# Decayed block attention followed by a two-layer MoE: attention by chunk over all heads, interleaved with both MoE layers on every engine; k transpose sharing the k-v matmul; smelu from one relu pass

## The chip, the cores and the metric

One core of one Trainium2 chip. The metric is the device time of the whole program in microseconds (us). An execution is timed several times; "span" is the length of one profiled execution, about 1.8 us shorter than the time of the same execution. Engines: PE (matmul), PEld (its weight loads), DVE (VectorE), ACT (ScalarE), POOL (GpSimd), SP (which here only asks for DMA transfers).

## The reference

```python
# attention: q, k, v are (4, 8, 768, 64) float32, lam one decay per head, near 1
for b in range(nb):                      # blocks of 64 tokens
    intra = (qb @ kb.T * Dmask) @ vb     # Dmask = lam ** (i - j) where i >= j, else 0
    inter = (qb * lam_pow) @ kv_state
    out[:, :, sl] = intra + inter
    kv_state = lam_block * kv_state + (kb * rev_pow).T @ vb
# MoE layer (one expert): x is (3072, 512)
h = x @ w_in                             # 512 -> 2048
g = np.where(h >= 1, h, np.where(h <= -1, 0.0, (h + 1) ** 2 / 4))   # smelu
y = g @ w_out                            # 2048 -> 512
```

The block size is free: the decay can be folded into q and k as powers of lam. Both kernels work on chunks of 128 tokens, in bfloat16 on PE.

## The kernel before

Attention runs first, one batch and one pair of heads at a time over all six chunks; only when all of x is there does the MoE run, in six stripes of 512 tokens. The framework's scheduler sets the order on each engine.

```python
    w_in_sb = big.tile([128, KO, d_ff], BF16)
    nc.gpsimd.dma_start(out=w_in_sb, in_=...)           # both weights, whole, first of all
    w_out_sb = big.tile([128, FO, d_model], BF16)
    nc.gpsimd.dma_start(out=w_out_sb, in_=...)
    ...
        for b in range(B):
            for hp in range(H // 2):                    # 16 head pairs
                # load q, k, v of the pair; scale q and k on ACT; k again on DVE
                # 12 PE transposes of 128x128, copied back by DVE
                kvp = kvpool.tile([128, 128], BF16, name="kvp", tag="kv")   # running k-v state
                for g in range(NG):
                    # 4 score matmuls of 64 rows; DVE multiplies by the causal mask
                    for bi in range(GRP):
                        nc.tensor.matmul(po[:, bi, :, :], lhsT=v_bf[:, blk, :], rhs=sc[:, bi, :, :], ...)
                        # two matmuls of 128 columns with kvp, then
                        nc.tensor.matmul(pkv, lhsT=kdd2[:, blk, :], rhs=v_bf[:, blk, :], ...)
                        for hi in range(2):
                            nc.vector.scalar_tensor_tensor(out=kvp[...], in0=kvp[...],
                                scalar=lamblk[...], in1=pkv[...], op0=AX.mult, op1=AX.add)
    ...
        for ms in range(NMS):                           # 6 stripes of 512 tokens
            for ni in range(FO):                        # layer 1: 16 x 4 matmuls of 512 columns
                ...
                nc.scalar.activation(out=tt, in_=ph, func=AF.Relu, scale=0.5, bias=chalf[:, 0:1])
                nc.scalar.activation(out=cc, in_=ph, func=AF.Relu, scale=1.0, bias=cm1[:, 0:1])
                nc.vector.tensor_single_scalar(aa, tt, 1.0, AX.min)
                nc.vector.tensor_tensor(a2, aa, aa, op=AX.mult)
                nc.vector.tensor_tensor(gT[:, ni, :], a2, cc, op=AX.add)
            for msub in range(MSTRIPE // 128):          # layer 2: 4 x 16 matmuls of 512 columns
                ...
```

## Time and profile before

358.08 us, median of 3 runs (358.08 to 358.14). Three parts of the span:

| part | from, us | to, us | what limits it |
|---|---|---|---|
| loads | 0 | 44 | q and k behind both weights |
| attention | 44 | 174 | PE, DVE and the k-v state waiting for each other |
| MoE | 174 | 356 | PE, and DVE in layer 1: 29.5 us for each stripe |

From the page of the kernel before: busy time of each engine, then the span in 40 slices of 8.9 us, in tenths.

```profile
PE 293.7 (82%) x1504; PEld 135.5 (38%) x1504; DVE 222.2 (62%) x693; ACT 203.0 (57%) x403; POOL 29.5 (8%) x44
...
PE   0011668888888888888999999999999999999995
...
DVE  0010678888888888888588078248518807825850
ACT  7112625544445555532399199369649729937951
...
PEclk9999999999999999999999999999999999999999
DMA  7999999878777734431000200110020020011011
```

PE starts late, is at 8 with DVE at 8 through the attention, and at 9 in the MoE. The chain of waits of the kernel before, its first 45 us (start, length, what):

```profile
3.68 10.29 SPq L121
...
14.01 4.87 SPq L124
...
18.91 4.96 SPq L121
...
26.44 4.99 SPq L121
```

Lines 121 and 124 ask for q and k. SP's queue is blocked for up to 10.3 us at a time, while the two weight loads (both asked for by 4 us) hold the DMA engines, which the page shows at 9.

How fast PE really streams is not in its busy time; it is in the distance between starts. PE's timeline of the kernel before, at the end of the attention (start, length, instruction):

```profile
174.08 0.31 PE L192 MATMUL po<-qTp,kvp 128*128 128x128 bf16 x1
174.19 0.42 PE L185 MATMUL po<-sc,v_bf 128*128 128x256 bf16 x1
174.40 0.32 PE L196 MATMUL pkv<-v_bf,kdd_1917 128*128 128x128 bf16 x1
174.51 1.49 PE L227 MATMUL ph<-xT,w_in_sb 128*128 128x512 bf16 x3
```

The 128-column matmul takes 0.11 us to the next start, the 256-column one 0.21, three 512-column ones 1.28: half the rate of the MoE later, where starts of 512 columns are 0.216 us apart. The PEclk row stays at 9 through both. Last, the costs of the old activation, from the groups of the kernel before (busy us, mean ns of one, after the bar):

```profile
L236 ACT ACTIVATE cc<-ph,cm_82 128x512 bf16<-128x512 f32 x96 | 77.3, 806 | 0.0
L233 ACT ACTIVATE tt<-ph,chalf 128x512 bf16<-128x512 f32 x96 | 76.7, 799 | 1.0 <-PE ph L227 0.9
L239 DVE TENSOR_SCALAR aa<-tt 128x512 bf16<-128x512 bf16 x96 | 27.6, 287 | 51.5 <-ACT tt L233 51.5
```

These lengths overlap: two passes start 0.57 us apart. Per 512 columns of layer 1, ACT needs 1.14 us and DVE 1.19 us, PE 0.86.

### The profile page before, as it was taken

What the parts mean: (1) busy time and instruction counts of PE and PEld (TensorE: products, weight loads), DVE (VectorE), ACT (ScalarE), POOL (GpSimd) and SP (SyncE); (2) the same over time, 40 slices, a digit from 0 to 9 for tenths busy, and PEclk for the clock granted to TensorE, in tenths of its full rate; (3) what the DMA queues carried; (4) which work ended last, traced back from release to release, by engine and by line L of the source; (5) the groups of instructions that cost most, each with busy time, mean ns of one, the idle gap of its engine ahead of it and who ended that gap; (6) DMA issues with size and microseconds to landing.
All of it is one profiled execution on the core that took longest, in us unless ns stands there. A gap on an engine that the chain in (4) does not pass through costs nothing.

```text
span 356.3 us, 4688 instructions
## 1 busy us (share of the span) xinstructions
PE 293.7 (82%) x1504; PEld 135.5 (38%) x1504; DVE 222.2 (62%) x693; ACT 203.0 (57%) x403; POOL 29.5 (8%) x44
## 2 busy tenths in 40 slices
PE   0011668888888888888999999999999999999995
PEld 0010334444444444443443443344344344344432
DVE  0010678888888888888588078248518807825850
ACT  7112625544445555532399199369649729937951
POOL 7000011111222221110000000000000000000000
PEclk9999999999999999999999999999999999999999
DMA  7999999878777734431000200110020020011011
GB/s 144 201 196 178 205 205 204 129 111 120 110 112 110 111 26 27 28 23 14 2 0 0 90 30 0 62 59 0 29 90 1 0 90 30 0 61 60 0 53 66
DMA packets 81481, 26.53 MB, mean 74 GB/s; under 512 B 75824, under 2 KB 77872, under 8 KB 81456
## 3 DMA queue, kind: packets, MB, share of 16 engines
q1 hardware_dynamic: 53776, 18.88, 23.6%
q0 software_dynamic: 27680, 7.34, 20.5%
q8 instruction: 12, 0.20, 0.2%
q14 instruction: 13, 0.11, 0.1%
HBM read 27.27 MB, written 6.29 MB: 94 GB/s over the span
## 4 chain that ended last, share of the span: by engine, by line
DVE 40%; PE 33%; SPq 11%; ACT 8%; issue 5%; DMA 1%; DVEq 0%; ACTq 0%
PE py L247 19%; DVE kvp L200 11%; DVE gT L242 8%; SPq L121 7%; PE po L185 5%; DVE aa L239 4%; ACT cc L236 4%; SPq L124 4%; DVE sc L177 3%; PE po L189 3%; PE psc L172 3%; ACT tt L233 3%; DVE kTp L158 3%; DVE qTp L158 2%; PE po L192 2%
## 5 line engine op out<-in xcount | busy, mean ns | idle before, releaser
L247 PE MATMUL py<-w_out_sb,gT 128*128 128x512 bf16 x384 | 93.8, 380 | 2.6 <-DVE gT L242 2.2
L227 PE MATMUL ph<-xT,w_in_sb 128*128 128x512 bf16 x384 | 94.0, 385 | 0.7
L236 ACT ACTIVATE cc<-ph,cm_82 128x512 bf16<-128x512 f32 x96 | 77.3, 806 | 0.0
L233 ACT ACTIVATE tt<-ph,chalf 128x512 bf16<-128x512 f32 x96 | 76.7, 799 | 1.0 <-PE ph L227 0.9
L211 ACT CAST xT<-po 64x256 bf16<-64x256 f32 x96 | 35.1, 366 | 70.7 <-PE po L192 70.2
L239 DVE TENSOR_SCALAR aa<-tt 128x512 bf16<-128x512 bf16 x96 | 27.6, 287 | 51.5 <-ACT tt L233 51.5
L227 PEld LDWEIGHTS <-w_in_sb 128*128 128x128 bf16 x384 | 37.8, 99 | 50.1 <-issue 10.8
L247 PEld LDWEIGHTS <-gT 128*128 128x128 bf16 x384 | 35.5, 98 | 53.5 <-DVE gT L242 14.0
L154 PE MATMUL ptr<-ident,qkdd 128*128 128x128 bf16 x192 | 30.6, 303 | 28.1 <-ACT qkdd L133 21.0
L253 ACT COPY osb<-py 128x512 f32<-128x512 f32 x24 | 13.9, 586 | 49.5 <-PE py L247 49.5
L172 PE MATMUL psc<-qTp,kTp 64*128 64x128 bf16 x192 | 30.9, 296 | 11.8 <-DVE kTp L158 7.2
L185 PE MATMUL po<-sc,v_bf 128*128 128x256 bf16 x96 | 35.9, 408 | 5.1 <-DVE sc L177 2.7
L177 DVE TENSOR_TENSOR sc<-psc,causalT 128x256 bf16<-128x256 f32 x96 | 37.7, 420 | 2.2
L127 POOL DMA_DIRECT2D v_bf<-in_v_dram x32 | 26.2, 827 | 129.4 <-PE pkv L196 117.2
L154 PEld LDWEIGHTS <-qkdd 128*128 128x128 bf16 x192 | 20.9, 136 | 35.2 <-ACT qkdd L133 21.2
L189 PE MATMUL po<-qTp,kvp 128*128 128x128 bf16 x80 | 23.6, 295 | 6.1 <-DVE kvp L200 5.1
L192 PE MATMUL po<-qTp,kvp 128*128 128x128 bf16 x80 | 25.1, 314 | 0.0
L172 PEld LDWEIGHTS <-kTp 64*128 64x128 bf16 x192 | 11.3, 106 | 32.5 <-issue 19.3
L189 PEld LDWEIGHTS <-kvp 128*128 128x128 bf16 x80 | 8.7, 109 | 22.7 <-DVE kvp L200 19.9
L185 PEld LDWEIGHTS <-v_bf 128*128 128x128 bf16 x96 | 10.6, 123 | 16.7 <-DVE sc L177 15.6
L158 DVE COPY qTp<-ptr 128x512 bf16<-128x512 bf16 (+1 forms) x32 | 11.3, 357 | 0.9
L158 DVE COPY kTp<-ptr 128x512 bf16<-128x512 bf16 (+1 forms) x32 | 11.1, 353 | 0.9 <-PE ptr L154 0.5
(326 smaller groups left out, 252.5 us busy)
## 6 DMA issues: line engine op xcount, KB each, us to landing
qk_nat<-in_q_dram SPq DMA_DIRECT2D x32, 192.0 KB, 4.0
qk_nat<-in_k_dram SPq DMA_DIRECT2D x32, 192.0 KB, 4.1
out_dram<-osb SPq DMA_DIRECT2D x24, 256.0 KB, 2.2
v_bf<-in_v_dram POOLq DMA_DIRECT2D x32, 96.0 KB, 3.3
w_in_sb<-in_moe_w_in_dram POOLq DMA_DIRECT2D x1, 2048.0 KB, 16.1
w_out_sb<-in_moe_w_out_dram POOLq DMA_DIRECT2D x1, 2048.0 KB, 28.3
lam_b<-in_lam_dram SPq DMA_DIRECT2D x1, 4.0 KB, 2.6
```

Source lines behind the costliest of these rows:

```text
L154: nc.tensor.transpose(out=ptr[:, c, :], in_=qkdd[:, base + c, off:off + 128], identity=ident)
L158: nc.vector.tensor_copy(dst[:, base:base + nchk, :], ptr[:, :nchk, :])
L172: nc.tensor.matmul(psc[:, bi, :], lhsT=kTp[ps:ps + 64, blk, :], rhs=qTp[ps:ps + 64, blk, :], start=True, stop=True)
L177: nc.vector.tensor_tensor(out=sc[:, :, hi, :], in0=psc, in1=_ins(causalT, 1, GRP), op=AX.mult)
L185: nc.tensor.matmul(po[:, bi, :, :], lhsT=v_bf[:, blk, :], rhs=sc[:, bi, :, :], start=True, stop=first)
L189: nc.tensor.matmul(po[:, bi, 0, :], lhsT=kvp, rhs=qTp[:, blk, :], start=False, stop=False)
L200: nc.vector.scalar_tensor_tensor(out=kvp[ps:ps + 64, ps:ps + 64], in0=kvp[ps:ps + 64, ps:ps + 64], scalar=lamblk[h0 + hi][ps:ps + 64, 0:1] ...
L227: nc.tensor.matmul(ph, lhsT=w_in_sb[:, ko, ni * 128:(ni + 1) * 128], rhs=xT[:, ko, m0:m0 + MSTRIPE], start=(ko == 0), stop=(ko == KO - 1))
L233: nc.scalar.activation(out=tt, in_=ph, func=AF.Relu, scale=0.5, bias=chalf[:, 0:1])
L236: nc.scalar.activation(out=cc, in_=ph, func=AF.Relu, scale=1.0, bias=cm1[:, 0:1])
L239: nc.vector.tensor_single_scalar(aa, tt, 1.0, AX.min)
L247: nc.tensor.matmul(py, lhsT=gT[:, ko, msub * 128:(msub + 1) * 128], rhs=w_out_sb[:, ko, :], start=(ko == 0), stop=(ko == FO - 1))
```

## The change

The intent is to have no attention phase at all. A unit of attention is one 128-token chunk and half the heads; there are 48. The first four chunks (8 units) run alone; the others are slotted between the MoE matmuls. All decay goes into two tables over the whole sequence, so the state U is a plain running sum. The order on every engine is written by hand. Both weights come in four slices each, after the first q, k and v. The matmul that makes the k-v product also transposes k: its moving operand is v beside an identity. The core of what is added (cut and shortened, with remarks; what it replaces is the code above):

```diff
+    ctx.enter_context(tc.manual_schedule())
...
+        nc.gpsimd.tensor_tensor(t, qf, _bc(tab_q[:, cb, :], 2, D), op=AX.mult)     # qs, on POOL
+        k_eng.tensor_tensor(t, kf, _bc(tab_k[:, cb, :], 2, D), op=AX.mult)         # ks: DVE for chunks 0-3, then POOL
+        nc.scalar.copy(out=vi[c % NV][:, :, 0, :], in_=vf...)                      # v beside the identity
+    def stage_t(u):        # 2 q transposes, 2 matmuls of 256 columns: k-v product and k transpose
+            nc.tensor.transpose(out=pq[:, j, :], in_=qs[c][...], identity=ident)
+            nc.tensor.matmul(pk[:, j], lhsT=ks[c][...], rhs=vi[c % NV][:, hp], start=True, stop=True)
+        # ACT: two copies of q into a block-diagonal tile, one of kT; DVE: U = U + pk
+    def stage_s(u):        # 2 score matmuls of 256 columns, DVE mask of 512
+    def stage_o(u):        # 2 or 4 matmuls of 256 columns, two ACT copies into xT
...
+        nc.scalar.activation(out=r_t[s][:, ni % 2, :], in_=ph, func=AF.Relu, bias=one[:, 0:1])
+        nc.vector.tensor_scalar(t, r, 0.5, 1.0, op0=AX.mult, op1=AX.min)           # per 1,024 columns
+        nc.vector.tensor_tensor(w, r, t, op=AX.subtract)
+        nc.vector.tensor_tensor(gT[s][:, ni - 1:ni + 1, :], w, t, op=AX.mult)
...
+    for c in range(CPS):                       # prologue: chunks 0 to 3
+        ensure_cast(c, nc.vector)
+        if c >= 1:
+            load_w_in(state["wi"]); state["wi"] += 1
+        # four attention steps
+    load_w_in(state["wi"])
+    for i in range(WS):
+        load_w_out(i)
+    ensure_loaded(CPS + 1)
+    ensure_cast(CPS)                           # chunk 4
+    # one more attention step: t of unit 8 and o of unit 7
...
+    for s in range(NST + 1):                   # step i: layer 1 of stripe s, layer 2 of stripe s - 1
+        for i in range(FO):
+            l1(s, i)            # 4 matmuls of 512 columns
+            # t or s of a unit
+            smelu(s, i)
+            l2(s - 1, i)        # 4 matmuls of 512 columns
+            # o of the unit before
```

## The prediction

> **What bounds it now.** The page and the timeline show three parts of the 356.3 us span. (a) To about 44 us: load-bound. The chain of waits is the sync queue's q and k issues (one blocked 10.3 us) while both weight loads hold the DMA engines; PE's first matmul is at 20.2 us. (b) 44 to 174 us: attention. PE and DVE are each busy about 88% (windows 60-150 us: PE 78.7, DVE 79.0 of 90), but PE, DVE and the running k-v state wait for each other. PE streams slowly: starts of 128-column matmuls are 0.107 us apart, of 256-column ones 0.21, of 512-column ones still 0.43 at 175 us. (c) 174 to 356 us: MoE, 29.5 us for each 512-token stripe. PE starts a 512-column matmul every 0.216 us, so 128 of them are 27.6 us; the rest is DVE (gT) not keeping up.
>
> The doubled spacing in (b) agrees with the Trainium skill, TensorE: Matmul & The Clock Gate, "What's actually happening": 1.2 GHz until sustained busy, then 2.4. The page's PEclk row does not show it.
>
> **What changes.** Attention runs in 48 units (a 128-token chunk, half the heads). A full unit is 2 transposes and 8 matmuls of 256 columns. At warm rate, estimated from the spacings above: 2 x 0.08 + 8 x 0.11 = 1.05 us, about 48 us in all, against 166 us for the MoE's 768 matmuls. All but the first 8 units are slotted between MoE matmuls, so part (b) ceases to be a phase and its waits are covered.
>
> Other engines, from the trace's spacings: ACT 0.57 us per 512 columns from PSUM, 0.37 per 256. One relu in place of two: 96 x 0.57 = 55; attention 5 x 0.37 + 0.3 = 2.15 per unit, 103; output copies 14: 172 us. DVE: smelu per 1,024 columns 0.42 + 2 x 0.69 = 1.8, 48 times = 86; masks 48 x 0.65 = 31; state 40 x 0.38 = 15; with setup 138 us. POOL: 44 products of 128x512; the Trainium skill, GPSIMD Engine Reference, "Elementwise — side-by-side cycle accounting" gives 2.6 cycles per element at 1.2 GHz: 1.1 us each, some 50 us in all, an estimate that this trace cannot check. So PE bounds the steady part.
>
> **Sum.** Prologue 31 us: first chunk ready near 9 us (q, k, v are issued before the weights), then 8 units at about 2.5 us, a serial ACT-PE-DVE chain on a cold PE, with chunk 3's load close behind. Stripe 0 (layer 1 and 9 units, no layer 2): ACT- and DVE-bound, 31. Stripes 1 to 3: 27.6 + 8 x 1.05, plus 4% for waits, 37.4 each, 112. Stripe 4: 36. Stripe 5, no attention: 28. Last layer 2: 14; last copy and store 4. Span 256; the measured time is 1.8 longer than the span now: **258 us**, range 247 to 275. Faster by over 2%: 0.98; within 2%: 0.01; slower: 0.01.
>
> **What would show it.** PE's first matmul near 9 us; first layer-1 matmul at 29 to 35 us; PE near 9 in every slice after it save stripe 0; 512-column starts 0.216 us apart throughout; ACT busy about 70%, DVE 55%; the chain mostly PE; POOL products 1.0 to 1.5 us.
>
> **What would make it wrong.** POOL products of 2 us or more, or shutting out DVE's two-input work (prologue and stripe 0 longer). PE falling back to the cold rate in stripe 0 (up to +15 us). Single PSUM buffers for pq, pk, ps and po stalling PE at each unit: 0.3 us x 40 is +12. First-layer weight slices queued behind q/k/v (the first slices late). A prologue unit nearer 3.5 us: +8.

## The result, and the profile after

The time is 263.36 us (median of 5 runs, 263.24 to 265.2), before 358.08 (357.62 to 358.14), result correct. The ratio is 0.737 (95% interval 0.735 to 0.739). Ratios are the mean time of one kernel's fast runs over that of the other's of the same rounds, so they are not quite the ratio of the medians quoted. The profiled execution is the slowest of the five (265.2 us, span 263.5); the others have spans of 261.5 to 262.2.

The page of the changed kernel, the same rows; a slice is now 6.6 us:

```profile
PE 222.8 (85%) x1209; PEld 118.7 (45%) x1232; DVE 143.8 (55%) x245; ACT 173.7 (66%) x389; POOL 54.2 (21%) x61
...
PE   0567306666889999999999999999999999999993
...
DVE  3554201388887576657574766574747645555300
ACT  4768303778996977797779777977796754554210
...
PEclk9999755999999999999999999999999999999998
DMA  6999999999990526753574357110111011111122
```

There is work from the first slice on, then a hole near slices 5 and 6 in PE, DVE and ACT together, then a stretch (slices 7 to 12) in which PE is at 6 to 8 while ACT rises from 3 to 9, and from slice 13 on PE is at 9 to the end. The hole in the merged timeline of the changed kernel (all engines; in brackets the idle time just before, and what ended it):

```profile
34.37 1.04 POOL L156 TENSOR_TENSOR ks<-kf,tab_k 128x512 bf16<-128x512 f32 x1 [7.35 <-DMA kf<-in_k_dram]
...
40.86 0.62 ACT L158 CAST vi_152<-vf 128x512 bf16<-128x512 f32 x1 [11.87 <-DMA vf<-in_v_dram]
...
41.53 0.58 PE L173 MATMUL pk<-vi_152,ks 128*128 128x256 bf16 x2 [12.56 <-ACT vi_152 L158]
...
43.19 1.62 PE L234 MATMUL ph<-xT,w_in_sb 128*128 128x512 bf16 x3 [0.22 <-issue]
```

PE stands for 12.6 us, ACT's copy of v of chunk 4 ends the wait, and that copy had itself waited 11.9 us for the load of v; k of the same chunk was 7.4 us late before it. This is attention step 17, the one the prologue has after its four chunks. Only then does layer 1 begin, at 43.2 us.

The steady part, PE's timeline of the changed kernel from one step to the second next:

```profile
88.84 1.03 PE L234 MATMUL ph<-xT,w_in_sb 128*128 128x512 bf16 x4
89.70 0.28 PE L169 MATMUL pq<-ident,qs 128*128 128x128 bf16 x2
89.81 0.38 PE L173 MATMUL pk<-vi_152,ks 128*128 128x256 bf16 x2
90.03 1.03 PE L258 MATMUL py<-w_out_sb,gT 128*128 128x512 bf16 x4
90.90 0.27 PE L206 MATMUL po<-qbd_146,U 128*128 128x256 bf16 x1
91.00 0.27 PE L207 MATMUL po<-sc,vi_150 128*128 128x256 bf16 x1
91.11 0.27 PE L206 MATMUL po<-qbd_146,U 128*128 128x256 bf16 x1
91.22 0.27 PE L207 MATMUL po<-sc,vi_150 128*128 128x256 bf16 x1
91.33 1.03 PE L234 MATMUL ph<-xT,w_in_sb 128*128 128x512 bf16 x4
92.20 0.38 PE L192 MATMUL ps<-qbd_148,kT 128*128 128x256 bf16 x2
92.41 1.03 PE L258 MATMUL py<-w_out_sb,gT 128*128 128x512 bf16 x4
```

No line has an idle time in brackets: every matmul starts when the one before it has been streamed. Two steps with one unit take 4.44 us (88.84 to 93.28): 16 matmuls of 512 columns at 0.216 are 3.45, and the unit is the other 0.99.

The groups that answer to those of the old activation, and POOL's products, in the changed kernel:

```profile
L238 ACT ACTIVATE r<-ph,one 128x512 bf16<-128x512 f32 x96 | 65.9, 687 | 43.3 <-PE ph L234 39.6
L153 POOL TENSOR_TENSOR qs<-qf,tab_q 128x512 bf16<-128x512 f32 x24 | 25.3, 1052 | 121.7 <-PE pq L169 92.0
...
L156 POOL TENSOR_TENSOR ks<-kf,tab_k 128x512 bf16<-128x512 f32 x20 | 22.3, 1117 | 7.9 <-DMA kf<-in_k_dram 7.9
```

One pass in place of two, and POOL at 1.04 to 1.1 us for each product.

Three times cut the span into the terms of the prediction: the first layer-1 matmul (end of the prologue), the first layer-2 matmul (within a microsecond of the start of stripe 1), and the end. All are starts of records in the traces.

| | first layer 1 | first layer 2 | end | prologue | stripe 0 | rest |
|---|---|---|---|---|---|---|
| predicted | 31 | 62 | 256 | 31 | 31 | 194 |
| the changed kernel | 43.2 | 79.1 | 263.5 | 43.2 | 35.9 | 184.4 |

The total hides two errors of opposite sign: the first two terms are 17 us too small together, the third 10 us too large.

### The profile page after: what moved, and what is told of

Same layout as the page of the kernel before. It is cut to its first block, busy times and chain, and to the rows that moved or that the text cites. A ratio compares the mean times of both kernels' runs of the same rounds, so it can differ in the third digit from the quotient of the medians.

```text
span 263.5 us, 3576 instructions
## 1 busy us (share of the span) xinstructions
PE 222.8 (85%) x1209; PEld 118.7 (45%) x1232; DVE 143.8 (55%) x245; ACT 173.7 (66%) x389; POOL 54.2 (21%) x61
## 4 chain that ended last, share of the span: by engine, by line
PE 69%; DVE 3%; ACT 1%; issue 0%; ACTq 0%
PE py L258 31%; PE ph L234 26%; PE po L207 3%; PE ps L192 3%; PE pk L173 2%; PE po L206 2%; PE pq L169 1%; DVE gT L250 1%; DVE w_726 L249 1%; DVE sc L195 0%; DVE w_768 L249 0%; ACT r L238 0%; DVE U L186 0%; ACT xT L212 0%; ACT osb L262 0%
## 5 line engine op out<-in xcount | busy, mean ns | idle before, releaser
L238 ACT ACTIVATE r<-ph,one 128x512 bf16<-128x512 f32 x96 | 65.9, 687 | 43.3 <-PE ph L234 39.6
L153 POOL TENSOR_TENSOR qs<-qf,tab_q 128x512 bf16<-128x512 f32 x24 | 25.3, 1052 | 121.7 <-PE pq L169 92.0
L186 DVE TENSOR_TENSOR U<-pk,U 128x256 bf16<-128x256 f32 x32 | 13.6, 424 | 56.5 <-ACT kT L179 56.5
L195 DVE TENSOR_TENSOR sc<-ps,causal 128x512 bf16<-128x512 f32 x48 | 32.9, 685 | 4.6 <-PE ps L192 4.0
L156 POOL TENSOR_TENSOR ks<-kf,tab_k 128x512 bf16<-128x512 f32 x20 | 22.3, 1117 | 7.9 <-DMA kf<-in_k_dram 7.9
L169 PE MATMUL pq<-ident,qs 128*128 128x128 bf16 x96 | 14.3, 235 | 6.7 <-POOL qs L153 6.7
L179 ACT CAST kT<-pk 128x256 bf16<-128x256 f32 x48 | 17.9, 372 | 2.4 <-PE pk L173 1.3
L173 PE MATMUL pk<-vi_152,ks 128*128 128x256 bf16 x32 | 6.8, 298 | 14.6 <-ACT vi_152 L158 12.6
L169 PEld LDWEIGHTS <-qs 128*128 128x128 bf16 x96 | 10.1, 106 | 16.8 <-POOL qs L153 6.7
L192 PEld LDWEIGHTS <-kT 128*128 128x128 bf16 x96 | 8.5, 101 | 19.4 <-ACT kT L179 11.0
L158 ACT CAST vi_152<-vf 128x512 bf16<-128x512 f32 x8 | 4.9, 610 | 11.9 <-DMA vf<-in_v_dram 11.9
L177 ACT COPY qbd_146<-pq 64x256 bf16<-64x256 bf16 x32 | 11.6, 361 | 1.6 <-PE pq L169 1.2
L177 ACT COPY qbd_144<-pq 64x256 bf16<-64x256 bf16 x32 | 11.5, 361 | 0.6 <-PE pq L169 0.2
L177 ACT COPY qbd_148<-pq 64x256 bf16<-64x256 bf16 x32 | 11.5, 361 | 0.5
```

What stands on the lines that cost most here:

```text
L153: nc.gpsimd.tensor_tensor(t, qf, _bc(tab_q[:, cb, :], 2, D), op=AX.mult)
L156: k_eng.tensor_tensor(t, kf, _bc(tab_k[:, cb, :], 2, D), op=AX.mult)
L169: nc.tensor.transpose(out=pq[:, j, :], in_=qs[c][:, 2 * hp:2 * hp + 2, :].rearrange("p a d -> p (a d)"), identity=ident)
L173: nc.tensor.matmul(pk[:, j], lhsT=ks[c][:, 2 * hp:2 * hp + 2, :].rearrange("p a d -> p (a d)"), rhs=vi[c % NV][:, hp], start=True, stop=True)
L177: nc.scalar.copy(out=qb[hi * 64:hi * 64 + 64, :, hi, :], in_=pq[hi * 64:hi * 64 + 64])
L179: nc.scalar.copy(out=t, in_=pk[:, :, 1, :])
```

## The experiments

Ten kernels were run. The first seven start from the changed kernel (263.36 us), the last three from the kernel before. A fourth run of the old activation (287.5 us) counts as slow and is left out. The stage times are those of one profiled execution each. For the changed kernel and the first run below it is the slowest of its runs, by about 2 us, and three runs with the same prologue and the same load order (old activation, k transpose apart, small POOL products) began layer 1 at 40.7 to 41.7 us and not 43.2. So a difference of 1 or 2 us between stage times is not read as an effect.

| run | median, us | ratio to before | first layer 1 | first layer 2 | end |
|---|---|---|---|---|---|
| second weights in stripe 0 | 255.2 | 0.715 | 33.2 | 71.2 | 255.6 |
| interleaving undone | 306.55 | 0.857 | 134.3 | 149.8 | 305.1 |
| old activation | 283.72 | 0.794 | 40.9 | 85.1 | 280.7 |
| k transpose apart | 262.97 | 0.735 | 41.7 | 76.9 | 261.5 |
| second weights later, less prefetch | 252.86 | 0.706 | 33.9 | 65.9 | 251.5 |
| small POOL products (wrong result) | 261.85 | 0.732 | 40.7 | 75.7 | 260.1 |
| first weights later as well | 253.65 | 0.710 | 28.8 | 67.3 | 251.6 |
| before, with the new activation | 349.11 | 0.975 | | | 346.8 |
| before, weights listed later | 350.47 | 0.979 | | | 348.6 |
| before, weights gated | 342.46 | 0.958 | | | 341.1 |

### Is the hole the weights' doing?

```diff
     load_w_in(state["wi"])
-    for i in range(WS):
-        load_w_out(i)
...
+            if s == 0 and i in (3, 5, 7, 9):
+                load_w_out((i - 3) // 2)
             if s < NST:
                 l1(s, i)
```

> The changed kernel with one edit: the four slices of the second weight matrix are asked for during stripe 0 (after its steps 3, 5, 7 and 9) and not before chunk 4's casts. Theory A (the 12.6 us in which PE waits for chunk 4's k and v, from 29 to 41.5 us, is their loads sharing the DMA engines with 6.3 MB of weights): the first layer-1 matmul moves from 43 us to about 31 to 34, and the time falls by 8 to 11 us, to about 253 to 255. Rival B (the loads are held by their own queue or by the rate of 256-byte pieces, whatever the weights do): the first layer-1 matmul stays at 41 us or later and the time within 2 us of 263. Rival C (the DMA time is only moved: stripe 0 then waits for chunks 5 to 8 and for the second weights): layer 1 starts early but stripe 1 starts at 76 to 79 us as now, and the time stays near 262.

Measured: 255.2 us (255.1 to 257.36, 4 runs), 8 us less. Layer 1 begins at 33.2 us and not 43.2. The waits of this run between 26 and 45 us (total, times, longest), against 12.6 us in the changed kernel:

```profile
PE pk L173 <- ACT vi L158: 3.4, 1, 3.4
PEld L173 <- POOL ks L156: 2.9, 1, 2.9
```

The same transfers, asked for from the same queue in the same order, land sooner when 4.2 MB of weights (2.1 MB once in bfloat16) don't compete with them. Theory A holds and B falls. The Trainium skill, DMA: Bandwidth & Descriptors, "Issuing engines are not separate DMA queues", says that transfers issued by different engines run on the same 16 DMA engines and interleave; the run agrees. C may be partly right: stripe 0 grew from 35.9 to 38.0 us, so about 2 of the 10 us came back there in these two profiles, no more than single profiles differ by.

### Is the interleaving what hides attention's waits?

```diff
     ensure_loaded(CPS + PF)
+    while state["att"] < NSUB:          # all attention first (xT kept for six stripes)
+        c = state["att"] // 4
+        ensure_loaded(c + PF)
+        ensure_cast(c + 1)
+        a, b_ = att_step()
+        for f in a + b_:
+            f()
```

> The changed kernel with the interleaving undone: all 48 attention units run before the first MoE matmul, in the same code, with the same loads (x tiles for all six stripes kept). If interleaving is what hides attention's waits (my prediction): 48 units at 2.3 to 2.6 us of a serial PE-ACT-DVE chain, plus the 12 us hole, is 120 to 135 us, then the MoE 6 x 27.7 us + 4: about 295 to 310. Rival (most of the gain is less work and earlier loads, interleaving is worth little): under 275.

Measured: 306.55 us (305.87 to 306.81), 43 us more than the changed kernel. Once the hole and the step after it are over, at 41.4 us, the 40 units that remain take until 134 us, 2.3 us each. In the windows view of this run (busy us with counts for PE, PEld, DVE, ACT, POOL; then granted clock, DMA share, GB/s):

```profile
43.00:134.00 91.00, 61.35 (x375) 34.04 (x374) 40.10 (x70) 80.22 (x214) 39.09 (x38) 0.85 0.93 162
```

ACT is busy 88% of it: alone, attention is held by ACT's five or six copies per unit, not by PE. The loads, which run at about 220 GB/s until 100 us, are not the bound either: between 120 and 134 us none is left (1 GB/s) and ACT is still busy for 12.73 of the 14 us. Interleaved, the same unit costs PE 0.99 us and its ACT work lies beside MoE matmuls. The MoE afterwards takes 171 us (134.3 to 305.1), 5 more than 768 matmuls at 0.2157 us.

### Is the one-pass activation worth more here than before?

```diff
-        nc.scalar.activation(out=r_t[s][:, ni % 2, :], in_=ph, func=AF.Relu, bias=one[:, 0:1])
+        nc.scalar.activation(out=tt, in_=ph, func=AF.Relu, scale=0.5, bias=chalf[:, 0:1])
+        nc.scalar.activation(out=cc, in_=ph, func=AF.Relu, scale=1.0, bias=cm1[:, 0:1])
...
+        nc.vector.tensor_single_scalar(aa, tt, 1.0, AX.min)
+        nc.vector.tensor_tensor(a2, aa, aa, op=AX.mult)
+        nc.vector.tensor_tensor(gT[s][:, ni, :], a2, cc, op=AX.add)
```

> The changed kernel with the old activation: two ScalarE passes of 0.57 us and three VectorE operations for each 512 columns. Per two MoE steps ACT then has 3.6 + 1.15 = 4.7 us and DVE about 3.5, against PE's 4.44. If ACT is what sets stripe 0 now (36 us, 16 passes more = +9) and becomes the bound of stripes 1 to 4 (+0.3 x 8 each): about +17 us, 278 to 284. Rival (the PE-bound stripes hide all of it, only stripe 0 pays): +9, 271 to 273. If the single pass is worth nothing because PE bounds everything: 263.

Measured: 283.72 us (282.39 to 285.74, the three fast runs), 20 us more, within the 278 to 284 expected. Stripe 0 grows by 8.3 us (to 44.2) and the rest by 11.2 (to 195.6). The windows view of this run:

```profile
90.00:225.00 135.00, 128.04 (x725) 66.18 (x723) 96.33 (x222) 128.42 (x281) 29.35 (x24) 1.00 0.34 81
```

and of the changed kernel in its steady part:

```profile
79.00:220.00 141.00, 140.16 (x801) 77.23 (x815) 88.81 (x154) 108.95 (x247) 24.87 (x24) 1.00 0.34 81
```

ACT goes from 77% busy to 95%. Its share of two steps (4.7 us, the estimate made before the run) passes PE's (4.44), and ACT becomes the bound: between 85 and 250 us PE waits 6.8 us for ACT's copy of k transposed, a wait that the changed kernel does not have there. The same swap in the kernel before is the first of the last three runs.

### Does the shared k transpose matter?

```diff
-            nc.tensor.matmul(pk[:, j], lhsT=ks[c][...], rhs=vi[c % NV][:, hp], start=True, stop=True)
+            nc.tensor.transpose(out=pq[:, 1, j, :], in_=ks[c][...], identity=ident)
+            nc.tensor.matmul(pk[:, j], lhsT=ks[c][...], rhs=vi[c % NV][:, hp, 0, :], start=True, stop=True)
```

> The changed kernel with the k transpose taken out of the k-v matmul: two transposes of 128 columns and two k-v matmuls of 128 columns in place of two of 256, so 512 columns for PE either way; four instructions in place of two per unit. If columns are what PE pays for (0.055 us per 128): within 0.5% of the changed kernel, 262 to 265. Rival (each matmul has a floor near 0.08 us from its weight load, as my prediction assumed): 2 x 40 units x 0.05 us = +4 us, 267.

Measured: 262.97 us (262.58 to 263.18); the rest of the span is 184.6 us against 184.4, so the rival (267) fails. Sharing the matmul buys no time: PE streams 512 columns a unit either way. It saves two pairs of PE instructions for each unit, no more.

### Is stripe 0 held by loads?

The edit is shown against the first of these runs (second weights in stripe 0), not against the changed kernel:

```diff
-            if s == 0 and i in (3, 5, 7, 9):
-                load_w_out((i - 3) // 2)
+            if s == 0 and i in (8, 10, 12, 14):
+                load_w_out((i - 8) // 2)
...
-    PF = 5
+    PF = 3
```

> The delayed second weights again, now asked for later still (steps 8, 10, 12 and 14 of stripe 0), and q, k, v loaded 3 chunks ahead in place of 5. In the run with delayed weights stripe 0 took 38 us with ScalarE busy 28.5 of it while the DMA engines moved 205 GB/s all through. If stripe 0 is now held by loads (theory): it falls to about 31 us, stripe 1 starts near 65 us, and the time is 248 to 250. If it is held by the engines alone (ACT order, PE falling cold, VectorE and POOL sharing a port): it stays at 36 us or more, and the time at 254 to 256.

Measured: 252.86 us (251.6 to 254.03), the fastest kernel. Stripe 0 takes 32.0 us (33.9 to 65.9), the 31 that the prediction had given it. ACT is then near its bound:

```profile
33.90:65.90 32.00, 26.20 (x157) 14.20 (x156) 24.42 (x38) 28.30 (x67) 15.27 (x16) 0.96 1.10 207
```

28.3 us of 32 busy. So up to 6 of the 38 us in the first of these runs were loads, asked for too early and in competition with each other; the two changes were made together, so what each gives is not known, and the medians differ by only 2.3 us. The time came out 3 us above the 248 to 250 that were expected, although stripe 1 began within 1 us of the 65 expected: 65, the rest of 184.4 and the 1.8 between span and time are 251 already, and the rest took 1.2 us more (185.6). Layer 1 still began at 33.9 us, after a wait for v of chunk 4.

### Is it POOL and DVE in each other's way?

In stripe 0 of the changed kernel, five of DVE's products have double length. Its DVE timeline:

```profile
71.13 1.41 DVE L249 TENSOR_TENSOR w_726<-r,t_724 128x1024 bf16<-128x1024 bf16 x1
72.58 1.42 DVE L250 TENSOR_TENSOR gT<-w_726,t_724 128x1024 bf16<-128x1024 bf16 x1
...
75.29 0.69 DVE L249 TENSOR_TENSOR w_768<-r,t_766 128x1024 bf16<-128x1024 bf16 x1
```

and its POOL timeline:

```profile
70.84 1.15 POOL L153 TENSOR_TENSOR qs<-qf,tab_q 128x512 bf16<-128x512 f32 x1 [4.01 <-PE pq L169]
71.96 1.49 POOL L156 TENSOR_TENSOR ks<-kf,tab_k 128x512 bf16<-128x512 f32 x1
```

The long ones lie on POOL's products. The Trainium skill, SBUF — State Buffer, "Who interferes with whom", says that a DVE instruction with two SBUF inputs and a POOL instruction that reads SBUF exclude each other; the trace agrees, with 0.72 us added for each of the seven collisions in the whole run. Whether it costs time is another matter. From chunk 5 on, POOL scales one head and not eight (wrong result: relative error 654):

```diff
-        nc.gpsimd.tensor_tensor(t, qf, _bc(tab_q[:, cb, :], 2, D), op=AX.mult)
+        nh = H if c <= CPS else 1          # the same for k; cut here: fixed tiles in place of the pool's
+        nc.gpsimd.tensor_tensor(t[:, :nh, :], qf[:, :nh, :], _bc(tab_q[:, cb, :nh], 2, D), op=AX.mult)
```

> Wrong result on purpose: from chunk 5 on, POOL scales only one head of eight (the rest of the tile keeps old numbers), so its products shrink from 1.04 us to about 0.2; all else is as in the changed kernel. If sharing a port with POOL is what makes stripe 0 long (five of its VectorE products took 1.41 us and not 0.69, together with the slower scalings some 4.5 us of DVE): no product of 1.41 us is left, stripe 0 falls from 36 to about 31 us and the time to 258 or 259. If the collisions are covered by ScalarE's 28.7 us and by the loads: the long products go but the time stays within 1.5 us, 262 to 264.

Measured: 261.85 us (261.85 to 262.3), just below the 262 to 264 of the second case. None of the 96 products is long any more and DVE's busy time falls by 5.6 us, but stripe 0 falls only from 35.9 to 35.0 us, no more than single profiles differ by: with the k transpose apart it was 35.2. That run has 18 long products in place of 7, and DVE is busy for 158.1 us in it in place of 143.8, at the same time of 263 us. The collisions are real, and a cost of them in time is not shown.

### Can the rest of the hole be had?

This edit is on top of the run with the second weights later and less prefetch (252.86 us):

```diff
-        if c >= 1:
+        if c >= 2:
             load_w_in(state["wi"])
...
-    load_w_in(state["wi"])
     ensure_loaded(CPS + 1)
     ensure_cast(CPS)
+    load_w_in(state["wi"])
+    load_w_in(state["wi"] + 1)
```

> The run with the second weights in steps 8 to 14 and 3 chunks of prefetch, and now also the first weights one chunk later each (first slice with chunk 2, the last two after chunk 4's casts). In the run it builds on, PE still waited about 5 us for chunk 4's v before layer 1, which began at 33.9 us. If that wait is the first weights' last two slices: layer 1 begins near 30 us and the time is 248 to 250. If the slices now come too late for layer 1, or the wait only moves: 251 to 254.

Measured: 253.65 us (252.96 to 254.59), no gain. Layer 1 begins at 28.8 us, so the 5 us were the first weights' slices. But stripe 0 then takes 38.5 us, with one wait of 6.7 us for a v load in it. The wait moved. The DMA engines move 212 GB/s through stripe 0 in this run, and 205 to 218 in the changed kernel and the two others with moved weights; no order of these transfers that was tried gets past that. That the rate of the loads is all that is left of the start is not shown: the nine chunks needed by the start of stripe 1 and both weights are 11.3 MB as written, by estimate 54 us at 210 GB/s, and stripe 1 begins at 66 to 67 us. The engines carry chunks fetched ahead as well, and ACT is busy for 28.3 to 28.8 us of stripe 0.

### How much did the activation and the load order give by themselves?

```diff
-                # kernel before: tt, cc on ACT; aa, a2, gT on DVE, per 512 columns
+                nc.scalar.activation(out=r[:, ni % 2, :], in_=ph, func=AF.Relu, bias=one[:, 0:1])
+                if ni % 2 == 1:
+                    nc.vector.tensor_scalar(t1, r, 0.5, 1.0, op0=AX.mult, op1=AX.min)
+                    nc.vector.tensor_tensor(w1, r, t1, op=AX.subtract)
+                    nc.vector.tensor_tensor(gT[:, ni - 1:ni + 1, :], w1, t1, op=AX.mult)
```

> The kernel before with only the activation changed to the single pass. Its MoE stripes took 29.5 us where PE needs 27.6: if ScalarE's and VectorE's 1.19 us per 512 columns is the cause, six stripes gain up to 1.7 us each: 347 to 350. If PE or something else sets the stripe: 356 to 358.

Measured: 349.11 us (348.53 to 349.58), 9 us less, as expected. In the chain of waits of this run a stripe is 28.0 us (the long layer-2 pieces start at 219.93 and 247.90), where it was 29.5. In the changed kernel the same swap was worth 20 us, because ACT there also carries the attention.

For the load order, both weight loads were first moved in the source to the sixth and the tenth head pair:

> The kernel before with only the weight loads moved: the first is asked for with the sixth head pair, the second with the tenth. If the first 44 us were load-bound because of the weights, the attention starts some 10 us in and the whole shifts by 20 to 28 us: 330 to 338. If the q, k and v loads are slow by themselves: over 350.

Measured: 350.47 us (350.33 to 350.75), 7.5 us less, which at the threshold of 2% counts as unclear. This run did not test what it was meant to. The kernel before leaves the order to the scheduler, which moved the loads back up: they are issued at 5.25 and 6.00 us, only behind the first pair's v. PE begins at 11.1 us and not 20.2, then stands for 15 us. So the loads were gated by data:

```diff
+                if b * (H // 2) + hp == 5:
+                    nc.gpsimd.tensor_copy(w_in_sb[:, 0, 0:1], v_bf[:, 0, 0:1])   # overwritten by the load
                     nc.gpsimd.dma_start(out=w_in_sb, in_=...)
```

> The kernel before with the weight loads truly held back: the last attempt only listed them later, and the scheduler moved them up to 5 us. Now a one-element copy from the sixth pair's v into the weight tile makes the first load wait for that v, and the same with the tenth pair for the second; the load overwrites it. If the early weights are what made the first 44 us load-bound: attention runs from about 11 us without the hole, and the time is 330 to 338. If attention is then held by its own loads or the weights delay it later just as much: over 345.

Measured: 342.46 us (341.6 to 344.06), 15 us less, and 4 us short of the expected range. The hole at the start is gone. But each whole weight load now delays the v loads behind it in the middle of the attention; from the waits of this run between 40 and 120 us:

```profile
PE pkv L201 <- DMA v_bf<-in_v_dram: 11.8, 2, 8.1
```

Two waits, 11.8 us together, which is the shortfall and more. The weight load in one piece stalled the loads behind it in either place; moving it only changed which.

## Why the prediction was right or wrong

The time, 263.4 us against 258, lies in the range of 247 to 275, and the direction was right. That the total is only 5 us off is partly luck: 17 us too few in the first two terms and 10 too many in the third.

- **What bounds the kernel before: right.** Weights held back give 15 us (gated run), the new activation 9 us. What it says of the attention between 44 and 174 us has no run of its own.
- **Attention ceases to be a phase, its waits are covered: right, and shown.** Undoing the interleaving alone costs 43 us, near half of the gain of 95.
- **The serial unit, "about 2.5 us": right,** 2.3 us each when run alone. The cause given was half right: on a chain of ACT, PE and DVE it is ACT that is 88% busy.
- **Prologue, "31 us: first chunk ready near 9 us ... with chunk 3's load close behind": the step that failed.** PE's first matmul is at 6.7 us, 2 us earlier than said, and steps 1 to 16 are through by 29.5 us. But the prologue ends with a seventeenth step, which needs k and v of chunk 4. These are asked for between 21 and 24 us, and so are (21.4 to 26 us) the last two slices of the first weights and all of the second. The prediction had the opposite danger among its warnings (weights late behind q, k and v). The term measured 43.2 us. Taking the second weights away from there makes it 33.2.
- **Stripe 0, "ACT- and DVE-bound, 31": undersized, 35.9 us.** ACT is busy for 28.7 us of it, which fits. Loads were not counted at all: with the second weights later and less prefetch it is 32.0. The rival that the prediction named, POOL shutting out DVE, changed stripe 0 by 0.9 us, which is not clear of the differences between profiles. A cold PE (starts at half rate) plays a part only in its first 3.5 us.
- **The rest, 194 us: oversized, 184.4.** The 4% allowed for waits, 4 us, is not there: single accumulator buffers never stall PE between 79 and 220 us (140.16 of 141 us busy). Transposes were put at 0.08 us each, which does not follow from the spacings given (half of 0.107 is 0.054); two of them take 0.11. A unit is 0.99 us and not 1.05, 2 us over the units that remain, and the terms hold 49 units (8, 9 and 32) where there are 48, 1 us more. Some 2 us of the 10 are not traced.
- **Busy times: right.** ACT 173.7 (172), DVE 143.8 (138), POOL's products 1.05 us (1.1).

What the other 52 us are, between the kernel before and the changed one with its interleaving undone (358 to 306.5), is only partly shown. The activation in the kernel before is 9 and the gated loads 15. The remaining 28 agree with the traces (before, the attention repeats every 8.55 us for each of 16 pairs, 137 us; the serial units are 48 x 2.3, 110), but no run changed the unit's form, the hand-written order or the slicing of the weights alone.

## What to carry to other kernels

Slot a latency-bound phase into a throughput-bound one, and check by sums per step that no second engine passes the first; it was the one-pass activation that kept ACT under PE. When a prologue is costed, list every transfer in the order in which it enters the DMA engines, with its bytes, up to the first step that needs it, since a prefetch that nothing needs yet delays the one that something does. And under a scheduler, read the order that it made: a load listed later need not be issued later.

## What the Trainium skill lacked or had wrong

- TensorE: Matmul & The Clock Gate, "Back-to-back issue gap", gives about 81 ns for a 128-column matmul in a stream of weight load and matmul pairs, and 131 for 512 columns. In the steady part here it is 56 ns for 128 (two transposes in 0.11 us), 109 for 256 and 216 for 512, each with its own weight load: its "isolated" formula fits and the "sustained" figures do not.
- The same page, "What's actually happening", on the two clock rates, agrees with the spacings (0.43 and 0.216 us). Its section "Seeing it yourself" warns that recorded clock events can't be fully trusted. The clock row of the profile can't be here either, whether or not for that reason: it is full in the changed kernel from 9 to 20 us and in the kernel before at 174 us, while starts were spaced at half rate.
- SBUF — State Buffer, "Who interferes with whom", has the exclusion, as an exclusive lock, but no measured duration for this pair: a product of 1,024 columns took 1.41 to 1.42 us in place of 0.69 in all seven collisions, and the POOL product up to 1.49 in place of 1.04. Stripe 0 was 35.0 us without them, and 35.9 and 35.2 us in two profiles with them.
- GPSIMD Engine Reference, "Elementwise — side-by-side cycle accounting": its 2.6 cycles per element gave 1.1 us; measured 1.04, with a broadcast second input and bfloat16 out.
- No page looked up gives what a mix of 256-byte pieces and weight slices reaches together: 187 to 226 GB/s, counted as written, in every slice from 7 to 79 us of the changed kernel.
